# Outputs of six expert blocks as rows, with seven products of sums in place of eight

## The chip, the cores and the metric

The kernel runs on one core of a Trainium2 chip. Its engines work side by side, each through its own list of instructions in order: TensorE (PE, matrix products into PSUM; PEld is its loading of weights), VectorE (DVE), ScalarE (ACT), GpSimd (POOL) and SyncE (SP), with sixteen DMA engines for transfers. The metric is the device time of one execution in microseconds (us), the median of several runs. A profile is one more execution, recorded by the hardware.

## The reference

The program has two stages. The first is a linear attention with decay (4 sequences of 768 tokens, 8 heads of 48); its output, 3072 tokens of 384 numbers, is the input `x` of the second. The second sends every token to one of eight experts, and this is the stage that the change touches:

```python
# D = 384, E = 8 experts, F = 1024 hidden units, all float32
e = fresh_e if s == 0 or local_gate[b, s] < 0.5 else prev_e     # the token's expert
h = np.maximum(x[b, s] @ w1[e], 0.0)                            # 384 -> 1024
out[b, s] = p[e] * (h @ w2[e])                                  # 1024 -> 384, times the gate
```

## The kernel before

The routing gives each expert a list of tokens. Two experts first get small units of 192 slots; then come eight blocks, one for each expert, sorted by size. Each unit gathers the rows of its tokens, turns them (so that features lie on the partitions), computes hidden units in eight groups `m` of 128, and accumulates the outputs in PSUM.

```python
BLOCKS = (448, 424, 392, 376, 352, 336, 232, 192)     # slots of the eight blocks
P, D, DK, FK = 128, 384, 3, 8

def turn(self, i, j):              # 128 gathered rows of unit i -> exT   (L1033, L1034)
    tp = self.bank("etp")[:, :D].rearrange("p (k t) -> p k t", k=DK)
    for kk in range(DK):
        nc.tensor.transpose(tp[:, kk, :n], u["xg"][j][:n, kk * P:(kk + 1) * P], ...)
    nc.vector.tensor_copy(u["xT"][:, :, j * P:j * P + n], tp[:, :, :n])

def hidden(self, i, m):            # (L1047, L1051); hps has two banks
    for kk in range(DK):
        nc.tensor.matmul(h[:, :n], lhsT=u["w1"][:, m, kk, :], rhs=u["xT"][:, kk, :], ...)
    nc.scalar.activation(u[m], h[:, :n], Act.Relu)

def output(self, i, m):            # outputs with features on partitions   (L1059)
    for d in range(DK):
        nc.tensor.matmul(u["y"][d][:, :n], lhsT=u["w2"][:, m, d * P:(d + 1) * P], rhs=u[m], ...)

def drain(self, i):                # one copy on ScalarE, two on VectorE    (L1096)
    for d in range(DK):
        (nc.scalar.copy if d == 0 else nc.vector.tensor_copy)(u["yT"][:, d], u["y"][d][:, :n])

def send(self, i, j):              # 128 slots turned back into rows, scaled, scattered
    tp = self.bank("otp")[:, :D].rearrange("p (k t) -> p k t", k=DK)
    for d in range(DK):
        nc.tensor.transpose(tp[:n, d], u["yT"][:, d, j * P:j * P + n], self.ident)      # L1103
    nc.vector.tensor_scalar(yo[:n], tp..., u["gate"][:n, c:c + 1], None, Alu.mult)      # L1105
    nc.gpsimd.indirect_dma_start(out=..., in_=yo[:n], ...)                              # L1106
```

`bank` takes one of two PSUM banks in turn. The order in which the instructions are issued is written by hand:

```python
for i in range(n):                                  # units
    for m in range(FK):
        self.hidden(i, m)
        if sends and (m >= 1 if i > EARLY else i == EARLY and m >= 4):
            self.send(*sends.pop(0))                # rows of the unit before
        if m and i == n - 1:
            self.rows(m - 1)                        # last block: rows directly
        elif m:
            self.output(i, m - 1)                   # one step behind the hidden group
        ...                                         # [cut: routing at certain steps]
        if FK - after <= m:
            self.turn(i + 1, m - (FK - after))      # inputs of the unit to come
    if i < n - 1:
        self.output(i, FK - 1)
        self.drain(i)
        sends += [(i, j) for j in range(len(u["rows"]))]
```

The last block of 192 slots already computes its outputs as rows: 128 slots with the hidden units as weights and `w2` as the moving operand of 384 columns (L1067), and the remaining 64 slots as two halves of 192 columns that go to the two halves of the partitions (L1074).

Of the kernel before, what the change touches and what calls it, by code (L numbers as in the profile page):

```python
# [31 lines left out]
ST = 4  # L32
# [8 lines left out]

BLOCKS = (448, 424, 392, 376, 352, 336, 232, 192)
HALF = BLOCKS[-1] - P

FRESH_TO = -1.5 * 2.0 ** -23

# [505 lines left out]
class Router:  # L552
# [271 lines left out]

    def halves(self):

        nc, c = self.nc, (E - 1) * ST + 1
        tok, self.gateh, self.sidh = self.tl("tokh", [P, 1]), self.tl("gateh", [P, 1]), self.tl("sidh", [P, 1], I32)
        for g in range(2):
            z = slice(g * HALF, (g + 1) * HALF)  # L830
            nc.vector.tensor_copy(tok[z], self.tok2[:HALF, c:c + 1])
            nc.vector.tensor_copy(self.gateh[z], self.gate[:HALF, c:c + 1])
        none = self.tl("noneh", [P, 1])
        nc.vector.scalar_tensor_tensor(none, tok, 0.0, self.big, Alu.is_equal, Alu.mult)
        nc.vector.scalar_tensor_tensor(none, tok, 2.0, none, Alu.mult, Alu.add)
        nc.vector.tensor_tensor(self.sidh, none, self.side, op=Alu.add)

    def head(self, bank):
        tok = self.tok0.rearrange("p e j -> p (e j)")
# [122 lines left out]
class Experts:  # L962

    def __init__(self, tc, st, x_d, w1, w2, out, ident, router):
        self.tc, self.nc = tc, tc.nc
        self.x_d, self.w1, self.w2, self.ident, self.router = x_d, w1, w2, ident, router
        r = router  # L970

        def unit(e, slots, first, gid, sid, gate):
            n = -(-slots // P)
            return dict(e=e, n=slots, cols=list(range(first, first + n)), gid=gid, sid=sid, gate=gate,
                        rows=[min(P, slots - j * P) for j in range(n)])

        self.units = [unit(e, HEAD, 2 * e, r.gid0, r.sid0, r.gate0.rearrange("p e j -> p (e j)")) for e in range(EARLY)]
        self.units += [unit(None, n, b * ST, r.gid, r.sid, r.gate) for b, n in enumerate(BLOCKS)]

        self.outs = dram_disjoint_views(out, sum(len(u["cols"]) for u in self.units))  # L980
        self.gp = st.enter_context(tc.tile_pool(name="gp", bufs=6))
        self.wps = [st.enter_context(tc.tile_pool(name="wp0", bufs=1, reuse_waits="tile"))]

    def open(self, st):
        def pool(name, bufs, **kw):
            return st.enter_context(self.tc.tile_pool(name=name, bufs=bufs, reuse_waits="tile", **kw))

        self.wps.append(pool("wp1", 1))
        self.xp = pool("xp", 2)
        self.hp = pool("hp", 3)  # L990
        self.yp = pool("yp", 4)
        self.op = pool("op", 4)
        self.yps = pool("yps", 1, space=PSUM)
        self.hps = pool("hps", 2, space=PSUM)
        self.tps = pool("tps", 2, space=PSUM)

    def bank(self, name):
        return self.tps.tile([P, 512], F32, name=name, tag="tp")

    def fetch(self, i, engine):  # L1000
        u, wp = self.units[i], self.wps[i % 2]
# [40 lines left out]
    def hidden(self, i, m):  # L1042
        nc, u = self.nc, self.units[i]
        n = u["n"]
        h = self.hps.tile([P, 512], F32, name="h")
        for kk in range(DK):
            nc.tensor.matmul(h[:, :n], lhsT=u["w1"][:, m, kk, :], rhs=u["xT"][:, kk, :],  # L1047
                             start=(kk == 0), stop=(kk == DK - 1))
        last = i == len(self.units) - 1
        u[m] = self.hp.tile([P, n], F32, name="hL" if last else "hT", tag="hL" if last else "hT", bufs=FK if last else 3)  # L1050
        nc.scalar.activation(u[m], h[:, :n], Act.Relu)  # L1051

    def output(self, i, m):
        nc, u = self.nc, self.units[i]
        n = u["n"]
        if m == 0:
            u["y"] = [self.yps.tile([P, 512], F32, name=f"y{d}") for d in range(DK)]
        for d in range(DK):
            nc.tensor.matmul(u["y"][d][:, :n], lhsT=u["w2"][:, m, d * P:(d + 1) * P], rhs=u[m],  # L1059
                             start=(m == 0), stop=(m == FK - 1))  # L1060

    def rows(self, m):

# [14 lines left out]
    def send_rows(self, half):  # L1078
        nc, u, r = self.nc, self.units[-1], self.router
        n = D // 2 if half else D  # L1080
        c = u["cols"][0]
        gate, sid = (r.gateh, r.sidh) if half else (u["gate"][:, c:c + 1], u["sid"][:, c:c + 1])
        out = self.outs.pop()
        yo = self.op.tile([P, n], F32, name="yo", tag="yo")
        nc.vector.tensor_scalar(yo, u["y"][half][:, :n], gate, None, Alu.mult)
        nc.gpsimd.indirect_dma_start(  # L1086
            out=out.rearrange("n (h d) -> (n h) d", h=2) if half else out,
            out_offset=bass.IndirectOffsetOnAxis(ap=sid, axis=0),
            in_=yo, in_offset=None, bounds_check=(2 * N if half else N) - 1, oob_is_err=False)

    def drain(self, i):
        nc, u = self.nc, self.units[i]
# [5 lines left out]
    def send(self, i, j):  # L1098
        nc, u = self.nc, self.units[i]
        n, c = u["rows"][j], u["cols"][j]  # L1100
        tp = self.bank("otp")[:, :D].rearrange("p (k t) -> p k t", k=DK)
        for d in range(DK):
            nc.tensor.transpose(tp[:n, d], u["yT"][:, d, j * P:j * P + n], self.ident)  # L1103
        yo = self.op.tile([P, D], F32, name="yo", tag="yo")
        nc.vector.tensor_scalar(yo[:n], tp[:n].rearrange("p d x -> p (d x)"), u["gate"][:n, c:c + 1], None, Alu.mult)  # L1105
        nc.gpsimd.indirect_dma_start(  # L1106
            out=self.outs.pop(), out_offset=bass.IndirectOffsetOnAxis(ap=u["sid"][:n, c:c + 1], axis=0),
            in_=yo[:n], in_offset=None, bounds_check=N - 1, oob_is_err=False)

    def routing(self, s):  # L1110

        r, bank = self.router, self.bank
        if s == 0:
            r.experts_of(1)
            r.shares(1)
            r.gates(0)
        if s == 1:
            r.keys(1, bank("kp1"))
            r.runs(1)
            r.powers(1)  # L1120
        if s == 2:
            r.turn_runs(1, bank("rp1"))
        if s == 3:
            r.last(1, bank("bc1"))
            r.one_hot(1)
        if s == 4:
            r.counts(1, [bank("rk1"), bank("tt1")])
            r.ranks(1)
            r.blocks()
            r.slots(1)  # L1130
            r.columns(1)
            r.numbers(1)
            r.places(1, 0)
            r.places(1, 1)
        if s == 5:
            self.fetch(EARLY, self.nc.sync)
        if s == 7:
            r.summed(1, 0)
            r.copied(0)
        if s == 8:  # L1140
            r.tokens(bank("tb1"))
            self.gather(EARLY)
            r.gates(1)
            r.weights(0)
            r.weights(1)
        if s == 10:
            r.summed(0, 1)
        if s == 12:
            r.summed(1, 1)
            r.copied(1)  # L1150
        if s == 2 * FK:
            r.ends(bank("tb2"))
        if s == 2 * FK + 4:
            self.flag()

    def run(self, att, flag, ready):
        self.flag = flag
# [9 lines left out]
        for i in range(n):  # L1167
# [5 lines left out]
            for m in range(FK):  # L1173
                self.hidden(i, m)
                if i == 0 and m == 0:
                    att.turn(B * HP - 1, [self.bank("tp") for _ in range(2)])
                if sends and (m >= 1 if i > EARLY else i == EARLY and m >= 4):
                    self.send(*sends.pop(0))
                if m and i == n - 1:
# [9 lines left out]
            if i < n - 1:  # L1189
# [52 lines left out]
def kernel(  # L1242
# [41 lines left out]
    with ExitStack() as st, tc.manual_schedule():  # L1284
# [6 lines left out]
        ex.open(st)  # L1291
        router.open(1, st.enter_context(tc.tile_pool(name="ro1", bufs=1)))

        def flag():
# [7 lines left out]
            fp = router.mp  # L1302
# [79 lines left out]
```

## Time and profile before

The time is 406.2 us, the median of three runs from 405.75 to 406.56.

| what | value |
|---|---|
| span of the profiled execution | 404.0 us, mean TensorE clock 0.997 |
| TensorE busy | 391.1 us (97%) |
| VectorE busy | 145.2 us (36%) |
| ScalarE busy | 72.9 us (18%) |
| the block of 448 slots | 157.6 to 196.9 us |
| the blocks of 424, 392, 376 | start at 196.9, 233.8, 267.7 us |
| the blocks of 352, 336, 232 | start at 300.3, 330.6, 359.3 us |
| the last block, 192 | 380 us to the end |

How to read it: a line of the timeline gives the start and the duration in us, the engine, the line of the program (L1059), the operation, what it writes and reads, the shape, and how many instructions were merged into it. A line of a group gives, after the bar, busy time in us and mean ns of one instruction, and after the next bar the idle time of that engine directly before these instructions and who ended it. The duration of a matmul contains its run through the array, which overlaps with that of the next; how many fit into a stretch is read from the distance of the starts.

### The profile page before, as it was taken

Reading aid. Unit: us, or ns where it says so; the run is one execution under the profiler, and the core shown is the slowest. Engines: PE = TensorE matmul, PEld = TensorE weight load, DVE = VectorE, ACT = ScalarE, POOL = GpSimd, SP = SyncE. Lnnn points to the kernel's source line nnn. Section 1 sums busy time; section 2 is a strip of 40 time slices with the busy share of each in tenths; the row PEclk is TensorE's granted clock in tenths of the full one; section 3 lists DMA queues with packets and bytes.
Section 4 is the critical chain, followed back from the end, with each engine's and each line's share of the span. In section 5 each row is a group of like instructions: output and inputs, shape, how many; then the busy total and the mean of one; then the engine's idle time right before and its main releaser. Section 6 shows DMA issues by size and latency. Waiting matters only on the chain. (4 is left out here: it accounts for less than half of the span.)

```text
span 404.0 us, 8246 instructions
## 1 busy us (share of the span) xinstructions
PE 391.1 (97%) x3427; PEld 277.7 (69%) x3427; DVE 145.2 (36%) x321; ACT 72.9 (18%) x176; POOL 143.3 (35%) x179
## 2 busy tenths in 40 slices
PE   7999999899999999999999999999999999999992
PEld 6777786777769997555555555566666666689972
DVE  7887567678753723222211111121121011021200
ACT  4132222222222211110111111010111011111110
POOL 8679998786030060011424012302302302202011
PEclk9999999999999999999999999999999999999998
DMA  7999998988028766201922261272244144162011
GB/s 258 410 409 409 407 378 301 331 294 318 5 62 309 311 230 222 117 19 31 328 90 72 83 264 39 61 270 85 67 178 174 54 181 171 41 255 110 0 36 34
DMA packets 17468, 74.90 MB, mean 185 GB/s; under 512 B 2734, under 2 KB 6591, under 8 KB 14864
## 3 DMA queue, kind: packets, MB, share of 16 engines
q1 hardware_dynamic: 10048, 56.89, 37.2%
q0 software_dynamic: 3424, 9.54, 7.3%
q10 hardware_dynamic: 3952, 7.87, 5.3%
q8 instruction: 29, 0.48, 0.5%
q14 instruction: 15, 0.12, 0.1%
HBM read 64.85 MB, written 9.54 MB: 184 GB/s over the span
## 5 line engine op out<-in xcount | busy, mean ns | idle before, releaser
L1047 PE MATMUL h<-exT,w1t 128*128 128x192 f32 (+7 forms) x480 | 138.8, 428 | 0.0
L1059 PE MATMUL y<-hT,w2t 128*128 128x192 f32 (+7 forms) x432 | 131.3, 440 | 0.0
L1047 PEld LDWEIGHTS h<-exT,w1t 128*128 128x128 f32 x480 | 86.3, 190 | 37.4 <-issue 14.8
L1059 PEld LDWEIGHTS y<-hT,w2t 128*128 128x128 f32 x432 | 77.3, 190 | 31.9 <-issue 13.2
L1106 POOL DMA_INDIRECT out_dram<-yo,sid x27 | 26.8, 991 | 183.6 <-DVE yo L1105 159.7
L1051 ACT ACTIVATE hT<-h 128x192 f32<-128x192 f32 (+7 forms) x72 | 31.9, 443 | 199.6 <-PE h L1047 199.6
L1034 DVE COPY exT<-etp 128x384 f32<-128x384 f32 (+7 forms) x29 | 14.3, 495 | 98.4 <-PE etp L1033 98.4
L1105 DVE TENSOR_SCALAR yo<-otp,gate 128x384 f32<-128x384 f32 (+7 forms) x27 | 16.6, 616 | 91.6 <-PE otp L1103 91.6
L1020 POOL DMA_INDIRECT xg<-x_d,gid x29 | 29.7, 1023 | 45.7 <-DVE sm L869 25.8
L286 DVE TENSOR_TENSOR am<-pair,kept 128x768 f32<-128x768 f32 x32 | 30.1, 951 | 15.7 <-PE pair L284 15.2
L218 POOL TENSOR_TENSOR pd<-rk 128x384 f32<-128x384 f32 x32 | 31.9, 1020 | 3.1 <-DMA rk<-in_rk_dram 2.3
L293 PE MATMUL y<-am,kv 128*64 128x128 f32 x384 | 27.8, 278 | 1.9 <-issue 1.2
L214 POOL TENSOR_TENSOR ke<-kv,endT 128x288 f32<-128x288 f32 x32 | 25.0, 805 | 4.5 <-DMA kv<-in_kv_dram 3.5
L293 PEld LDWEIGHTS y<-am,kv 128*64 128x64 f32 x384 | 23.9, 136 | 3.0 <-issue 1.4
L231 POOL TENSOR_TENSOR rw<-rk,tab 128x384 f32<-128x384 f32 x26 | 23.6, 932 | 6.5 <-PE y L306 6.5
L284 PE MATMUL pair<-rw,kw 48*64 48x128 f32 (+1 forms) x768 | 22.5, 249 | 1.2 <-ACT end L165 0.6
L284 PEld LDWEIGHTS pair<-rw,kw 48*64 48x64 f32 x768 | 19.4, 133 | 2.6 <-issue 1.0
L310 ACT COPY xT<-y 128x768 f32<-128x768 f32 (+1 forms) x16 | 12.5, 779 | 40.7 <-PE y L306 40.7
L269 DVE TENSOR_TENSOR y<-y,vT 128x768 f32<-128x768 f32 x16 | 15.4, 962 | 3.7 <-PE y L265 3.5
L1033 PEld LDWEIGHTS etp<-ident,xg 128*128 128x128 f32 (+7 forms) x87 | 10.2, 140 | 8.2 <-issue 5.9
L238 DVE TENSOR_TENSOR kw<-rk,inv 128x768 f32<-128x768 f32 (+1 forms) x19 | 15.5, 818 | 0.1
L1103 PEld LDWEIGHTS otp<-ident,yT 128*128 128x128 f32 (+7 forms) x81 | 10.1, 132 | 7.7 <-issue 5.5
(214 smaller groups left out, 274.2 us busy)
## 6 DMA issues: line engine op xcount, KB each, us to landing
w1t<-in_w_dram SPq DMA_DIRECT2D x9, 1536.0 KB, 6.3
w2t<-in_w_dram SPq DMA_DIRECT2D x9, 1536.0 KB, 8.3
rk<-in_rk_dram SPq DMA_DIRECT2D x15, 768.0 KB, 9.3
kv<-in_kv_dram SPq DMA_DIRECT2D x16, 584.0 KB, 9.5
vT<-in_vT_dram SPq DMA_DIRECT2D x16, 384.0 KB, 7.5
x_d<-x ACTq DMA_DIRECT2D x4, 1152.0 KB, 11.3
w1t<-in_w_dram ACTq DMA_DIRECT2D x1, 1536.0 KB, 9.0
w2t<-in_w_dram ACTq DMA_DIRECT2D x1, 1536.0 KB, 12.3
```

The lines of the kernel that those rows point to most:

```text
L214: nc.gpsimd.tensor_mul(t["ke"][:, p::2], t["k"][:, p::2], spread(self.endT[:, p, hp], 1, C2))
L218: nc.gpsimd.tensor_mul(t["pd"][:, z], t["rT"][:, z], t["kT"][:, z])
L231: engine.tensor_mul(t["rw"][:, z], t["rT"][:, z], spread(pw, 1, z.stop - z.start))
L284: nc.tensor.matmul(sc[f * DP:(f + 1) * DP, h, i, x:], lhsT=t["kw"][q, c, o * DP:(o + 1) * DP], rhs=t["rw"][q, c, x:], start=True, stop=True)
L286: return lambda: nc.vector.tensor_mul(t["am"][:, g], sc, spread(self.kept[:, g:g + 3], 1, 2))
L293: nc.tensor.matmul(t["y"][p * DP:(p + 1) * DP, h, c2 * P:(c2 + 1) * P], lhsT=t["v"][:, (2 * c + h) * DH:(2 * c + h) * DH + DP], rhs=t["am" ...
L1020: self.nc.gpsimd.indirect_dma_start(out=xg[:n], out_offset=None, in_=self.x_d[:rows], in_offset=bass.IndirectOffsetOnAxis(ap=u["gid"][:n, ...
L1047: nc.tensor.matmul(h[:, :n], lhsT=u["w1"][:, m, kk, :], rhs=u["xT"][:, kk, :], start=(kk == 0), stop=(kk == DK - 1))
L1051: nc.scalar.activation(u[m], h[:, :n], Act.Relu)
L1059: nc.tensor.matmul(u["y"][d][:, :n], lhsT=u["w2"][:, m, d * P:(d + 1) * P], rhs=u[m], start=(m == 0), stop=(m == FK - 1))
L1105: nc.vector.tensor_scalar(yo[:n], tp[:n].rearrange("p d x -> p (d x)"), u["gate"][:n, c:c + 1], None, Alu.mult)
L1106: nc.gpsimd.indirect_dma_start(out=self.outs.pop(), out_offset=bass.IndirectOffsetOnAxis(ap=u["sid"][:n, c:c + 1], axis=0), in_=yo[:n], in ...
```

## The change

A product of two-by-two blocks, eight block products, can be made from seven, if sums of blocks are multiplied (Winograd's form of Strassen's scheme). The change uses it for the outputs of the six blocks of at least 336 slots: the first 256 slots in two halves of 128, the hidden groups in pairs, and the 384 output features in two halves of 192. The hidden units are the weights, so that the result has slots on the partitions, as rows. The slots beyond 256 are done in the ordinary way: as rows of 384 columns for up to 128 of them, as in the last block for 192 of them (448), and with features on the partitions, as before, for 168 and 136 of them (424 and 392). Rows need no turning back before they are scattered. What it is for: fewer columns through TensorE, and fewer transposes.

```diff
+PAIRS = 336
-        self.op = pool("op", 4)
+        self.op = pool("op", 5)
+        self.sp = pool("sp", 2)
+        self.jp = pool("jp", 1)
-        self.tps = pool("tps", 2, space=PSUM)
+        self.tp = [tps.tile([P, 512], F32, name=f"tp{i}") for i in range(2)]
     def bank(self, name):
-        return self.tps.tile([P, 512], F32, name=name, tag="tp")
+        if self.both:
+            self.tp.reverse()
+        return self.tp[0]                  # one bank from the first large block on
+    def sums(self, i, j):                  # four on VectorE, 128 x 128
+        for x, (a, b, op) in enumerate(((a21, a22, Alu.add), (t[:, 0], a11, Alu.subtract),
+                                        (a11, a21, Alu.subtract), (a12, t[:, 1], Alu.subtract))):
+            nc.vector.tensor_tensor(t[:, x], a, b, op=op)
+    def factors(self, i, j):               # four on VectorE, 128 x 192, of w2
+        for x, (a, b) in enumerate(((b12, b11), (b22, t[:, 0]), (b22, b12), (t[:, 1], b21))):
+            nc.vector.tensor_tensor(t[:, x], a, b, op=Alu.subtract)
+    def seven(self, i, j):                 # [cut]
+            u["hr"], u["y"] = y[3][:, half:D], self.tp[1]      # the rest takes the other bank
+        rest(m)
+        product(1, u[m][:, :P], h[:, m, :half])
+        rest(m + 1)
+        product(2, u[m + 1][:, :P], h[:, m + 1, :half])
+        product(4, u[m + 1][:, P:2 * P], t[:, 3])
+        product(5, s[:, 0], t[:, 0])
+        product(6, s[:, 1], t[:, 1])
+        product(7, s[:, 2], t[:, 2])
+        product(3, s[:, 3], h[:, m + 1, half:])
+    def join(self, i):                     # after the last pair
+        nc.scalar.copy(one, p(1))
+        nc.vector.tensor_tensor(u6, p(6), one, op=Alu.add)
+        ...                                # six more of 128 x 192 on VectorE
+        for x in range(2):
+            self.scaled(i, x, c[x], c[x])
+        if n <= P or n == P + HALF:
+            self.scaled(i, 2, u["y"][:, :D], ...)
+        ...                                # [cut: half rows of 448; yT of 424 and 392 on ScalarE]
+    def scaled(self, i, j, rows, yo):
+        self.nc.scalar.activation(yo[:n], rows[:n], Act.Copy, scale=u["gate"][:n, c:c + 1])
+        self.scatter(yo[:n], u["sid"][:n, c:c + 1])
@@ the order of issue
+                if u["seven"]:
+                    if m % 2:
+                        self.sums(i, m // 2)
+                        self.seven(i, m // 2)
+                        if m < FK - 1:
+                            self.factors(i, m // 2 + 1)
+                elif m and i == n - 1:
@@ [turn(i + 1, ...) follows here as before]
+            if i + 1 < n and self.units[i + 1]["seven"]:
+                self.factors(i + 1, 0)
+                self.both = False
+            if u["seven"]:
+                self.join(i)
+                if "yT" in u:
+                    sends += [(i, j) for j in range(2, len(u["rows"]))]
```

The indices and gates of half rows, which VectorE prepares at the end of the routing with seven small instructions for the last block, are now prepared for the 448 block too. A check on the decay values (`flag`), which used a bank of its own (`router.mp`), takes the bank for transposes, since `router.mp` now holds one of the seven products. The hidden tiles of the large blocks get four buffers (eight in the 448 block) in place of three.

More of the change, by code (lines that the diff above doesn't have):

```diff
@@ L825, in halves @@
     def halves(self):
[L827 to L836, printed above, removed]
+        nc, self.halved = self.nc, {}
+        for b in (0, E - 1):
+            c = b * ST + -(-BLOCKS[b] // P) - 1
+            tok, none = self.tl(f"tokh{b}", [P, 1]), self.tl(f"noneh{b}", [P, 1])
+            gate, sid = self.halved[b] = self.tl(f"gateh{b}", [P, 1]), self.tl(f"sidh{b}", [P, 1], I32)
+            for g in range(2):
+                z = slice(g * HALF, (g + 1) * HALF)
+                nc.vector.tensor_copy(tok[z], self.tok2[:HALF, c:c + 1])
+                nc.vector.tensor_copy(gate[z], self.gate[:HALF, c:c + 1])
+            nc.vector.scalar_tensor_tensor(none, tok, 0.0, self.big, Alu.is_equal, Alu.mult)
+            nc.vector.scalar_tensor_tensor(none, tok, 2.0, none, Alu.mult, Alu.add)
+            nc.vector.tensor_tensor(sid, none, self.side, op=Alu.add)
     def head(self, bank):
@@ L974, in unit @@
             return dict(e=e, n=slots, cols=list(range(first, first + n)), gid=gid, sid=sid, gate=gate,
+                        seven=slots >= PAIRS, rest=slots - 2 * P,
                         rows=[min(P, slots - j * P) for j in range(n)])
@@ L991, in open @@
         self.yp = pool("yp", 4)
-        self.op = pool("op", 4)
+        self.op = pool("op", 5)
+        self.sp = pool("sp", 2)
+        self.jp = pool("jp", 1)
         self.yps = pool("yps", 1, space=PSUM)
         self.hps = pool("hps", 2, space=PSUM)
-        self.tps = pool("tps", 2, space=PSUM)
+        tps = pool("tps", 1, space=PSUM)
+        self.tp = [tps.tile([P, 512], F32, name=f"tp{i}") for i in range(2)]
+        self.both = True
     def bank(self, name):
-        return self.tps.tile([P, 512], F32, name=name, tag="tp")
+        if self.both:
+            self.tp.reverse()
+        return self.tp[0]
     def fetch(self, i, engine):
@@ L1048, in hidden @@
                              start=(kk == 0), stop=(kk == DK - 1))
-        last = i == len(self.units) - 1
-        u[m] = self.hp.tile([P, n], F32, name="hL" if last else "hT", tag="hL" if last else "hT", bufs=FK if last else 3)
+        last = i == len(self.units) - 1 or u["seven"] and u["rest"] == P + HALF
+        u[m] = self.hp.tile([P, n], F32, name=f"hL{n}" if last else "hT", tag=f"hL{n}" if last else "hT", bufs=FK if last else 4)
         nc.scalar.activation(u[m], h[:, :n], Act.Relu)
@@ L1060, in output @@
                              start=(m == 0), stop=(m == FK - 1))
+    def sums(self, i, j):
+        nc, u = self.nc, self.units[i]
+        (a11, a21), (a12, a22) = [[u[2 * j + k][:, x * P:(x + 1) * P] for x in range(2)] for k in range(2)]
+        u["s"] = t = self.sp.tile([P, 4, P], F32, name="sums")
+        for x, (a, b, op) in enumerate(((a21, a22, Alu.add), (t[:, 0], a11, Alu.subtract),
+                                        (a11, a21, Alu.subtract), (a12, t[:, 1], Alu.subtract))):
+            nc.vector.tensor_tensor(t[:, x], a, b, op=op)
@@ new lines, in factors, with product, rest @@
+    def factors(self, i, j):
+        nc, u = self.nc, self.units[i]
+        (b11, b12), (b21, b22) = [[u["w2"][:, 2 * j + k, x * D // 2:(x + 1) * D // 2] for x in range(2)] for k in range(2)]
+        u["t", j] = t = self.sp.tile([P, 4, D // 2], F32, name="factors")
+        for x, (a, b) in enumerate(((b12, b11), (b22, t[:, 0]), (b22, b12), (t[:, 1], b21))):
+            nc.vector.tensor_tensor(t[:, x], a, b, op=Alu.subtract)
+    def seven(self, i, j):
+        nc, u = self.nc, self.units[i]
+        n, h, half = u["rest"], u["w2"], D // 2
+        if j == 0:
+            y = [self.yps.tile([P, 512], F32, name=f"y{d}") for d in range(DK)] + [self.router.mp]
+            u["p"] = {k: (y[x // 2], x % 2) for x, k in enumerate((1, 2, 4, 5, 6, 7, 3))}
+            u["hr"], u["y"] = y[3][:, half:D], self.tp[1]
+        def product(k, a, b):
+            bank, x = u["p"][k]
+            nc.tensor.matmul(bank[:, x * half:(x + 1) * half], lhsT=a, rhs=b, start=(j == 0 and x == 0),
+                             stop=(j == FK // 2 - 1), skip_group_check=True)
+        def rest(m):
+            first, last = m == 0, m == FK - 1
+            if n <= P or n == P + HALF:
+                z = min(n, P)
+                nc.tensor.matmul(u["y"][:z, :D], lhsT=u[m][:, 2 * P:2 * P + z], rhs=h[:, m], start=first, stop=last)
+            else:
+                for d in range(DK):
+                    nc.tensor.matmul(u["y"][:, d * n:(d + 1) * n], lhsT=h[:, m, d * P:(d + 1) * P], rhs=u[m][:, 2 * P:],
+                                     start=(first and d == 0), stop=last, skip_group_check=True)
+        m, s, t = 2 * j, u["s"], u["t", j]
+        rest(m)
[7 more added lines that the diff above has]
+        product(3, s[:, 3], h[:, m + 1, half:])
+        if j == FK // 2 - 1 and n == P + HALF:
+            for m in range(FK):
+                for g in range(2):
+                    nc.tensor.matmul(u["hr"][g * HALF:(g + 1) * HALF], lhsT=u[m][:, 3 * P:],
+                                     rhs=h[:, m, g * half:(g + 1) * half], start=False, stop=(m == FK - 1), skip_group_check=True)
@@ new lines, in join, with p @@
+    def join(self, i):
+        nc, u = self.nc, self.units[i]
+        n, half = u["rest"], D // 2
+        def p(k):
+            bank, x = u["p"][k]
+            return bank[:, x * half:(x + 1) * half]
+        t = self.jp.tile([P, 3, half], F32, name="t")
+        c = [self.op.tile([P, D], F32, name="yo", tag="yo") for _ in range(2)]
+        one, u6, z = t[:, 0], t[:, 1], t[:, 2]
+        nc.scalar.copy(one, p(1))
+        nc.vector.tensor_tensor(u6, p(6), one, op=Alu.add)
+        nc.vector.tensor_tensor(c[0][:, :half], p(2), one, op=Alu.add)
+        nc.vector.tensor_tensor(z, p(7), u6, op=Alu.add)
+        nc.vector.tensor_tensor(u6, p(5), u6, op=Alu.add)
+        nc.vector.tensor_tensor(c[1][:, :half], z, p(4), op=Alu.subtract)
+        nc.vector.tensor_tensor(c[1][:, half:], p(5), z, op=Alu.add)
+        nc.vector.tensor_tensor(c[0][:, half:], p(3), u6, op=Alu.add)
+        for x in range(2):
+            self.scaled(i, x, c[x], c[x])
+        if n <= P or n == P + HALF:
+            self.scaled(i, 2, u["y"][:, :D], self.op.tile([P, D], F32, name="yo", tag="yo"))
+            if n > P:
+                yo, (gate, sid) = self.op.tile([P, D], F32, name="yo", tag="yo")[:, :half], self.router.halved[i - EARLY]
+                nc.scalar.activation(yo, u["hr"], Act.Copy, scale=gate)
+                self.scatter(yo, sid, True)
+        else:
+            u["yT"] = self.yp.tile([P, DK, n], F32, name="yT", tag="yT")
+            nc.scalar.copy(u["yT"].rearrange("p d n -> p (d n)"), u["y"][:, :DK * n])
@@ new lines, in scaled, with scatter @@
+    def scaled(self, i, j, rows, yo):
+        u = self.units[i]
+        n, c = u["rows"][j], u["cols"][j]
+        self.nc.scalar.activation(yo[:n], rows[:n], Act.Copy, scale=u["gate"][:n, c:c + 1])
+        self.scatter(yo[:n], u["sid"][:n, c:c + 1])
+    def scatter(self, yo, sid, half=False):
+        out = self.outs.pop()
+        self.nc.gpsimd.indirect_dma_start(
+            out=out.rearrange("n (h d) -> (n h) d", h=2) if half else out,
+            out_offset=bass.IndirectOffsetOnAxis(ap=sid, axis=0),
+            in_=yo, in_offset=None, bounds_check=(2 * N if half else N) - 1, oob_is_err=False)
@@ L1081, in send_rows @@
         c = u["cols"][0]
-        gate, sid = (r.gateh, r.sidh) if half else (u["gate"][:, c:c + 1], u["sid"][:, c:c + 1])
-        out = self.outs.pop()
-        yo = self.op.tile([P, n], F32, name="yo", tag="yo")
+        gate, sid = r.halved[E - 1] if half else (u["gate"][:, c:c + 1], u["sid"][:, c:c + 1])
+        yo = self.op.tile([P, D], F32, name="yo", tag="yo")[:, :n]
         nc.vector.tensor_scalar(yo, u["y"][half][:, :n], gate, None, Alu.mult)
[L1086 to L1089, printed above, removed]
+        self.scatter(yo, sid, half)
     def drain(self, i):
@@ L1101, in send @@
         tp = self.bank("otp")[:, :D].rearrange("p (k t) -> p k t", k=DK)
+        first = j * P - (2 * P if u["seven"] else 0)
         for d in range(DK):
-            nc.tensor.transpose(tp[:n, d], u["yT"][:, d, j * P:j * P + n], self.ident)
+            nc.tensor.transpose(tp[:n, d], u["yT"][:, d, first:first + n], self.ident)
         yo = self.op.tile([P, D], F32, name="yo", tag="yo")
         nc.vector.tensor_scalar(yo[:n], tp[:n].rearrange("p d x -> p (d x)"), u["gate"][:n, c:c + 1], None, Alu.mult)
-        nc.gpsimd.indirect_dma_start(
-            out=self.outs.pop(), out_offset=bass.IndirectOffsetOnAxis(ap=u["sid"][:n, c:c + 1], axis=0),
-            in_=yo[:n], in_offset=None, bounds_check=N - 1, oob_is_err=False)
+        self.scatter(yo[:n], u["sid"][:n, c:c + 1])
     def routing(self, s):
@@ L1153, in routing @@
         if s == 2 * FK + 4:
-            self.flag()
+            self.flag(bank("fp"))
     def run(self, att, flag, ready):
@@ L1178, in run @@
                     self.send(*sends.pop(0))
-                if m and i == n - 1:
+                if u["seven"]:
[5 more added lines that the diff above has]
+                elif m and i == n - 1:
                     self.rows(m - 1)
@@ L1188, in run @@
                     self.turn(i + 1, m - (FK - after))
-            if i < n - 1:
+            if i + 1 < n and self.units[i + 1]["seven"]:
[5 more added lines that the diff above has]
+                    sends += [(i, j) for j in range(2, len(u["rows"]))]
+            elif i < n - 1:
                 self.output(i, FK - 1)
@@ L1292, with flag @@
         router.open(1, st.enter_context(tc.tile_pool(name="ro1", bufs=1)))
-        def flag():
+        def flag(fp):
             ok = ro.tile([P, 2, HP], F32, name="ok")
@@ L1301, in flag @@
             nc.vector.tensor_reduce(some, ok[:, 0], axis=AX.X, op=Alu.add)
-            fp = router.mp
             nc.tensor.matmul(fp[:1, :1], lhsT=some, rhs=router.ones[:, 0:1], start=True, stop=True)
```

## Prediction

> **What bounds the kernel now.** I read the page first (busy shares, then the 40 slices), then the groups by line with shapes kept apart, then the waits, then the timeline of single stretches. The chain of waits was no help: it has two pieces, both at the very end.
>
> ```profile
> PE 391.1 (97%) x3427; PEld 277.7 (69%) x3427; DVE 145.2 (36%) x321; ACT 72.9 (18%) x176; POOL 143.3 (35%) x179
> PE   7999999899999999999999999999999999999992
> ...
> L1059 PE MATMUL y<-hT,w2t 128*128 128x192 f32 (+7 forms) x432 | 131.3, 440 | 0.0
> L1105 DVE TENSOR_SCALAR yo<-otp,gate 128x384 f32<-128x384 f32 (+7 forms) x27 | 16.6, 616 | 91.6 <-PE otp L1103 91.6
> ```
>
> TensorE is busy 97% of the span and the output matmuls (L1059) have 0.0 us of idle time in front of them, while VectorE and ScalarE wait for TensorE. So any time taken from TensorE's stream comes off the end, and any wait put into it is added. A matmul of the program appears as two records (10 units x 8 x 3 hidden matmuls give x480). A busy TensorE is not yet TensorE at its pace, so I took the pace from the distance between starts.
>
> ```profile
> 219.89 2.30 PE L1059 MATMUL y<-hT,w2t 128*128 128x424 f32 x6
> 222.02 0.49 PE L1033 MATMUL etp<-ident,xg 128*128 128x128 f32 x3
> 222.35 2.30 PE L1047 MATMUL h<-exT,w1t 128*128 128x424 f32 x6
> 222.55 0.56 DVE L1034 COPY exT<-etp 128x384 f32<-128x384 f32 x1 [4.04 <-PE etp L1033]
> ...
> 389.08 0.81 PE L1067 MATMUL y<-w2t,hL 128*128 128x384 f32 x2
> 389.72 1.14 PE L1047 MATMUL h<-exT,w1t 128*128 128x192 f32 x6
> 390.70 0.81 PE L1067 MATMUL y<-w2t,hL 128*128 128x384 f32 x2
> ```
>
> Six records of 424 columns take 222.02 - 219.89 = 2.13 us (0.356 each), six of 192 take 0.98 (0.163), two of 384 take 0.64 (0.32), a group of three transposes 0.33. All lie on p(n) = 0.833 n + 3 ns. There is no minimum at 192 columns: the 190 ns of a weight load are hidden. VectorE's copy of transposes starts 0.53 us after the first of them, 0.2 us after their last slot.
>
> ```profile
> 194.22 0.38 PE L1033 MATMUL etp<-ident,xg 40*128 40x40 f32 x3
> 194.53 2.52 PE L1059 MATMUL y<-hT,w2t 128*128 128x448 f32 x6
> 196.89 3.37 PE L1047 MATMUL h<-exT,w1t 128*128 128x424 f32 x9
> ```
>
> This is the border of two blocks. Between the last transposes of the next block's inputs and the first hidden matmul that reads them lie 2.36 us of output matmuls, which hide the copy. Keep this in mind.
>
> [...]
>
> **The change part by part.**
>
> *Columns.* Before, outputs of a block of n slots are 48 records of n columns: 48 p(n) = 18.06, 17.10, 15.82, 15.18, 14.22, 13.58 us for n = 448 to 336, sum 94.0. After: seven products x 4 pairs x 2 records = 56 records of 192, 56 x 0.163 = 9.13 us a block, 54.8 for six. (The 256 slots alone cost 48 x 0.833 x 256 = 10.24 before, so a block gains 1.1.) The rest of the slots: for 376, 352 and 336 16 records of 384 columns whatever the number of slots, 5.17 us each, against 4.80, 3.84 and 3.20 for 120, 96 and 80 slots; for 424 and 392 48 records of 168 and 136 columns, 6.86 and 5.58; for 448 5.17 plus 32 half-width records, which in the last block now take (2.82 - 0.33)/31 = 0.08 us each because two run side by side, 2.6. Sum 35.7. Total 90.5: the products win only **3.4 us**, because 352 and 336 lose what they win.
>
> *Transposes of outputs.* Row outputs need no turning back: 4 + 2 + 2 + 3 + 3 + 3 = 17 of 27 groups go, 17 x 0.33 = **5.6 us**. Gain in TensorE's stream together: **9.0 us**.
>
> *Border, first wait (A).* In the built order of the changed kernel, the last transposes of the next block's inputs stand directly before its first hidden matmul, because the seven products of the last pair are issued before them and nothing remains for afterwards. So TensorE waits 0.2 us (to the copy's start) + copy + about 0.17 (signal and weight load). The copies are 0.28 us for 40 slots and 0.18 for 8 in the trace; for 120, 96, 80 and 104 slots I read 0.53, 0.45, 0.40, 0.47 from the 0.36 and 0.56 at 64 and 128 slots. Sum over six borders 6 x 0.37 + 2.3 = **4.5 us**.
>
> *Border, second wait (B).* ScalarE takes the scaling of three row groups into its queue ahead of the next block's first Relu. [...] Counting from the transposes' last slot, with c the copy: sums complete at 0.2 + c + 1.3 + 2.25 = c + 3.75; ScalarE's scaling 0.6 + 0.5 + 0.5 to c + 5.4 (448 has a fourth, c + 5.8); Relu 0.4, signal 0.2: c + 6.0. TensorE meanwhile has only two hidden groups after wait A, ready at c + 0.37 + 12 p(n'): c + 4.65 for 424, 4.66 and 4.5 for 392 and 376 (with one send), 3.9 and 3.8 for 352 and 336. The border to 232 has no factors: c + 4.6 against c + 2.7. Waits 1.8, 1.35, 1.4, 2.05, 2.2, 1.85: **10.6 us**. Before, one ScalarE copy and two VectorE copies were all, and two hidden groups hid them.
>
> *Inside the 448 block (C).* Its first sums stand behind the routing's end on VectorE, which runs to 164.17 us in the trace and gets 1.0 us longer; the fifth product is due at 162.23 + 2.28 = 164.5 and gets its sum near 165.65: 1.15. With one transpose bank, the flag's matmul waits for the send's scaling and four small operations, and the next transposes for the flag's reader: 0.2 + 1.16 + 0.15 + 0.3 + 0.15 + 0.15 - 0.1 = 2.0. At the seventh step a send and a turn meet in the bank: 0.95. Together **4.1 us**.
>
> [...]
>
> Sum: -9.0 + 4.5 + 10.6 + 4.1 = **+10.2 us**, 406.2 + 10.2 = 416.4.
>
> **The rivals.** First: the gain arrives whole, since TensorE was the bound and VectorE is idle in these blocks (its digit is 0 to 2 in most slices): 397 us. Against it stands the built order, in which TensorE's next work needs a copy that begins only then. Second: the join is hidden as drains are today and only A and C are paid: 406.2 - 9.0 + 8.6 = 406. For it: 3.4 to 4.3 us of hidden matmuls at each border. [...]
>
> **Range and chances.** The gain is sure to about 1 us, A and C to 1.5 each. B is weakest: 0.5 us more or less per border moves the result by 3, and it could fall to half if neighbours overlap more than I count. I predict **416 us**, 80% between **409** and **421**. Faster by over 2% (below 398) would need no wait at all: 0.06. Slower by over 2% (above 414.3): 0.6. Within 2%: 0.34.
>
> **What would show it.** Right: the six first hidden groups have 0.5 to 0.9 us of TensorE idle before them, released by VectorE's exT; the first rest matmul of the next block has 1.3 to 2.2 us, released by ScalarE's hT; the 448 block shows gaps near its fifth product and at the flag; paces stay on p(n). Wrong: gaps at borders under 1 us in sum (then B is hidden), 192-column products slower than 0.17 us each, or gaps inside every pair.

## The result and the profile after

The changed kernel took 410.5 us (median of 4 runs, 410.0 to 411.3) against 406.1 us of the kernel before (median of 4): a ratio of 1.0109, 95% interval 1.0088 to 1.0131. It is slower by 4.4 us, 1.1%. The prediction had said 416 us, slower by 10.2 us.

The page of the changed kernel, engines, slices and the TensorE groups of the blocks (in the slices each digit is the busy share of a fortieth of the span, in tenths; in the groups the last figures are the idle time before and who ended it):

```profile
PE 384.6 (94%) x3616; PEld 298.5 (73%) x3616; DVE 191.5 (47%) x533; ACT 80.4 (20%) x195; POOL 143.8 (35%) x179
...
PE   7999999999999999989899999989989989989992
...
L1061 PE MATMUL h<-exT,w1t 128*128 128x192 f32 (+7 forms) x480 | 138.2, 429 | 2.9 <-DVE exT L1048 2.9
...
L1074 PE MATMUL y<-hT,w2t 128*128 128x192 f32 (+1 forms) x144 | 29.3, 340 | 1.2 <-ACT hT L1066 1.2
L1106 PE MATMUL y<-factors,sums 128*128 128x192 f32 x144 | 27.4, 327 | 0.7 <-DVE sums L1084 0.7
...
L1113 PE MATMUL tp<-w2t,hT 128*120 128x384 f32 (+2 forms) x48 | 19.7, 491 | 2.8 <-ACT hT L1066 2.8
```

TensorE is busy for 6.5 us less than before (384.6 against 391.1), although it has 189 records more, and the span is 4.3 us longer. Eights stand among its nines, in the half of the span where the blocks lie. The idle time in front of its groups, 0.0 before, now has names: VectorE's copy of inputs (exT), ScalarE's Relu (hT), VectorE's sums. All TensorE waits from the 448 block on, longest first (total us, times, longest):

```profile
PE h L1061 <- DVE exT L1048: 2.9, 6, 0.6
PE tp L1113 <- ACT hT L1066: 2.8, 2, 1.5
PE tp L1429 <- DVE some L1428: 1.2, 1, 1.2
PE y L1074 <- ACT hT L1066: 1.2, 1, 1.2
PE tp L1219 <- ACT yT L1165: 1.2, 2, 0.7
PE tp L1116 <- ACT hT L1066: 1.0, 1, 1.0
PE tp L1047 <- DVE yo L1221: 0.7, 1, 0.7
PE y L1106 <- DVE sums L1084: 0.7, 1, 0.7
PE tp L1047 <- DVE over L1430: 0.2, 1, 0.2
```

Six waits for the copy and six for ScalarE (2 + 1 + 2 + 1) are the two waits at each of the six borders. At 424 to 392 and 392 to 376 the one that waits for ScalarE is a send of the block before: its transposes need `yT`, which ScalarE copies after the two scalings and ahead of the Relu. The other four are inside the 448 block: the flag, its reader, the send that shares the bank, the first sums. These figures leave out the last record's own run through the array (a record of 192 columns lasts 0.33 us, the next one starts after 0.16), during which no new record starts, so the loss is larger than their sum of 11.9 us.

How long each block lasts, from its first hidden matmul to that of the next (the last column ends with TensorE's last record):

| kernel | 448 | 424 | 392 | 376 | 352 | 336 | 232 and 192 | all |
|---|---|---|---|---|---|---|---|---|
| before | 39.28 | 36.94 | 33.90 | 32.58 | 30.30 | 28.73 | 37.2 | 238.95 |
| after | 42.10 | 36.08 | 33.89 | 32.78 | 31.66 | 30.96 | 37.8 | 245.31 |

The 448, 352 and 336 blocks lose, 424 wins a little, 392 stays, 376 loses slightly. In sum the part of the program that changed is **6.4 us** longer, not 4.4. The profiled executions differ by 2.0 us ahead of it: the 448 block starts at 157.61 us before and at 155.58 after. The first experiment looks at that.

One border in the changed kernel's timeline, 376 to 352 (start and duration in us):

```profile
299.46 0.41 PE L1047 MATMUL tp<-ident,xg 96*128 96x96 f32 x3
...
299.91 0.46 DVE L1048 COPY exT<-tp 128x288 f32<-128x288 f32 x1 [2.23 <-PE tp L1047]
300.29 0.35 DVE L1092 TENSOR_TENSOR factors<-w2t 128x192 f32<-128x192 f32 x1
300.43 3.82 PE L1061 MATMUL h<-exT,w1t 128*128 128x352 f32 x12 [0.55 <-DVE exT L1048]
...
301.49 0.35 DVE L1148 TENSOR_TENSOR t<-y,t 128x192 f32<-128x192 f32 x1
...
303.20 0.35 DVE L1154 TENSOR_TENSOR yo<-mp,t 128x192 f32<-128x192 f32 x1
303.58 1.12 ACT L1171 ACTIVATE yo<-yo,gate 128x384 f32<-128x384 f32 x2 [5.23 <-DVE yo L1154]
...
304.61 0.56 ACT L1171 ACTIVATE yo<-tp,gate 120x384 f32<-120x384 f32 x1
305.07 0.80 ACT L1066 ACTIVATE hT<-h 128x352 f32<-128x352 f32 x2
305.57 0.89 PE L1113 MATMUL tp<-w2t,hT 128*96 128x384 f32 x2 [1.33 <-ACT hT L1066]
```

Read it as one chain: transposes, copy, four factors (300.29 to 301.49), seven additions of the join (to 303.55), three scalings (to 305.07), the Relu that had long been possible, and only then TensorE again. TensorE has two groups of hidden matmuls in the meantime, which end near 304.1.

### The profile page after: what moved, and what is told of

The parts are those of the page before. It is cut to its first block, busy times and chain, and to the rows that moved or that the text cites. A ratio compares the mean times of both kernels' runs of the same rounds, so it can differ in the third digit from the quotient of the medians.

```text
span 408.3 us, 8809 instructions
## 1 busy us (share of the span) xinstructions
PE 384.6 (94%) x3616; PEld 298.5 (73%) x3616; DVE 191.5 (47%) x533; ACT 80.4 (20%) x195; POOL 143.8 (35%) x179
## 5 line engine op out<-in xcount | busy, mean ns | idle before, releaser
L1061 PEld LDWEIGHTS h<-exT,w1t 128*128 128x128 f32 x480 | 85.3, 190 | 35.6 <-issue 12.7
L1066 ACT ACTIVATE hT<-h 128x192 f32<-128x192 f32 (+6 forms) x64 | 26.8, 428 | 140.9 <-PE h L1061 140.9
L1048 DVE COPY exT<-tp 128x384 f32<-128x384 f32 (+7 forms) x29 | 14.3, 494 | 68.0 <-PE tp L1047 68.0
L1084 DVE TENSOR_TENSOR sums<-hT 128x128 f32<-128x128 f32 x40 | 11.5, 288 | 60.3 <-ACT hT L1066 60.3
L1074 PE MATMUL y<-hT,w2t 128*128 128x192 f32 (+1 forms) x144 | 29.3, 340 | 1.2 <-ACT hT L1066 1.2
L1106 PE MATMUL y<-factors,sums 128*128 128x192 f32 x144 | 27.4, 327 | 0.7 <-DVE sums L1084 0.7
L1074 PEld LDWEIGHTS y<-hT,w2t 128*128 128x128 f32 x144 | 24.9, 190 | 2.0 <-ACT hT L1066 1.6
L1106 PEld LDWEIGHTS y<-factors,sums 128*128 128x128 f32 x144 | 24.0, 190 | 1.0 <-DVE sums L1084 1.0
L1113 PE MATMUL tp<-w2t,hT 128*120 128x384 f32 (+2 forms) x48 | 19.7, 491 | 2.8 <-ACT hT L1066 2.8
L1106 PE MATMUL y<-w2t,hT 128*128 128x192 f32 x80 | 19.6, 326 | 0.0
```

The costliest lines, as they stand in the source:

```text
L1106: nc.tensor.matmul(bank[:, x * half:(x + 1) * half], lhsT=a, rhs=b, start=(j == 0 and x == 0), stop=(j == FK // 2 - 1), skip_group_check=True)
```

## The experiments

The traces give a measure that is far finer than the times: the lengths of undisturbed blocks repeat to 0.01 or 0.02 us from one execution to the next, while the times of one kernel spread by several us on some chips (20 runs of one variant on one chip: 408.0 to 413.3 us). So each variant is judged by its ratio to the kernel before on the same chip, and by the lengths of its blocks.

**The two kernels again.** No edit.

> The kernel before, unchanged, once more. It settles a side question: the profile of before has TensorE waiting 1.2 us for nothing visible at 73.4 us, in the attention stage, which the profile of the changed kernel has not; its expert blocks start 2.0 us earlier. If that pause belongs to the kernel before (its own build), it is there again at the same place and the 448 block starts near 157.6 us. If it was chance of one execution, the block starts near 155.6 us and the pause is gone, and the changed kernel's loss is 2 us larger than its blocks alone explain.

> The changed kernel, unchanged, beside its variants on one chip. In the traces the six blocks last 201.7 us before (twice, to 0.01 us) and 207.5 after, and the rest of TensorE's work after them 37.2 and 37.8: 6.4 us in sum, while the times differ by 4.4. If the missing 2.0 us were an advantage of the changed kernel in the attention stage, the ratio is again 1.011. If they were chance of the few runs, it comes nearer to 1.016.

Measured: the kernel before again lasts 238.95 us from the first hidden group of 448 to TensorE's end, and its block starts at 161.14 us. Neither of the two expected starts came. It paused in other places: TensorE waited in front of L293 for 0.57 us at 72.73 us and 2.15 us at 114.19 us, and once in the first experts. The first line is from the first execution of the kernel before, the second from the repeat:

```profile
73.44 1.47 PE L293 MATMUL y<-am,kv 128*64 128x128 f32 x20 [1.19 <-issue]
```

```profile
150.78 1.24 PE L1059 MATMUL y<-hT,w2t 128*128 128x192 f32 x6 [2.03 <-ACT hT L1051]
```

The first pause is shorter and the second is new, in the same code. Over all twelve profiled executions of this study the 448 block starts between 155.6 and 163.4 us, and the start goes with the chip more than with the kernel: 155.8 to 157.7 us on one chip, 160.1 to 160.4 on a second, 161.1 to 163.4 on a third. A difference of 2.0 us is within what one chip shows. With four runs of the changed kernel and fifteen of the kernel before on one chip the changed one stands at 1.0166 (1.0133 to 1.02), 411.4 us against 405.1, and its blocks repeat: 42.08, 36.08, 33.89, 32.78, 31.67, 30.96. What has to be explained is 6.4 us; the ratio of 1.0109 was probably low by the 2 us by which the two executions differ ahead of the blocks. What makes the pauses is open.

**The last transposes ahead of the last products**, at all borders but 448 to 424.

```diff
+                early = u["seven"] and m == FK - 1 and i > EARLY
+                if early:
+                    self.turn(i + 1, m - (FK - after))
                 if u["seven"]:
                     if m % 2:
                         self.sums(i, m // 2)
...
-                if FK - after <= m:
+                if FK - after <= m and not early:
```

> The last transposes of the next block's inputs are issued ahead of the seven products of the last pair, at five of the six borders. Theory (both waits at a border are one chain: copy of exT, factors, join, scaling, Relu): the first wait goes and VectorE makes the factors under the products, so that the second wait shrinks too; each border gains 1.1 to 1.5 us, the last 0.45: 5.5 us, 405.0. Rival (the waits are independent): only the first wait goes, 3.0 to 3.5 us, 407. Second rival (the second wait is counted from the last product, whatever the copy does): the first wait passes into the second and nothing is gained, 410.5.

Measured: ratio 0.9975 (0.9949 to 1.0); first hidden group of 448 to TensorE's end 238.31 us, 7.0 less than the changed kernel, where 5.5 had been expected. At the five borders the first waits are gone; of the second ones those of 424 to 392 and 392 to 376 are gone, those of 376 to 352 and 352 to 336 shrink, and the one before 232, where no factors are made, stays. The same border in this kernel:

```profile
303.52 0.49 PE L1106 MATMUL mp<-w2t,sums 128*128 128x192 f32 x2
303.79 0.36 DVE L1148 TENSOR_TENSOR t<-y,t 128x192 f32<-128x192 f32 x1 [0.74 <-PE y L1106]
303.84 3.71 PE L1061 MATMUL h<-exT,w1t 128*128 128x352 f32 x12
...
307.88 0.89 PE L1113 MATMUL tp<-w2t,hT 128*96 128x384 f32 x2 [0.33 <-ACT hT L1066]
```

The factors are made under the products, and the join's first addition now waits for TensorE (0.74 us), the other way round than before. It starts before the last product (mp) is through, since it needs only the sixth and the first. From the end of the last product's slot (303.84) to TensorE's restart pass 4.04 us; in the changed kernel 5.14 us pass from its first hidden group to the restart (300.43 to 305.57). Both waits are one chain; the two rivals (3.5 us, nothing) fall.

**The join ahead of the factors.**

```diff
             if i + 1 < n and self.units[i + 1]["seven"]:
-                self.factors(i + 1, 0)
                 self.both = False
             if u["seven"]:
                 self.join(i)
+            if i + 1 < n and self.units[i + 1]["seven"]:
+                self.factors(i + 1, 0)
+            if u["seven"]:
```

> The join stands ahead of the next block's four factors on VectorE; nothing else is changed. Theory (the second wait is the chain through VectorE): sums are complete 1.2 us earlier, the waits of 1.14, 0.8, 0.87, 1.48 and 1.63 us shrink to 0 to 0.4, the border to 232 stays as it is: 5.2 us, 405.3. Rival (ScalarE's four or five operations alone make the wait, VectorE is done in time): no change, 410.5. Possible price: the factors come late for the fourth product, which would show as a wait for VectorE there.

Measured: ratio 1.0000 (0.9974 to 1.0026), 239.82 us, 5.5 less than the changed kernel's 245.31. The second waits are gone but for idle times of 0.13 us at the border to 352, 0.27 at that to 336 and the unchanged 1.23 before 232; no wait for factors appears. VectorE's place in the chain is real: the four factors take 1.2 us ahead of the join, and the 352 and 336 blocks, whose second waits were longer than that, are each 1.20 us shorter (30.47 and 29.76).

**The scaling behind the Relus.**

```diff
-        for x in range(2):
-            self.scaled(i, x, c[x], c[x])
+        self.late = [lambda x=x: self.scaled(i, x, c[x], c[x]) for x in range(2)]
...
+                if m == 1:                       # after hidden(i, 1) and its Relu
+                    for what in self.late:       # the half rows of 448 come first
+                        what()
+                    self.late = []
```

> ScalarE scales the two joined row groups (and the half rows of 448) only after the next block's first two Relus; the remaining rows, which need no join, are scaled at once. Theory (the second wait is the Relu's place in ScalarE's queue behind work that waits for VectorE): the second waits of 7.3 us in sum go, plus about 0.5 for weight loads after a wait; 403.0. Rival (TensorE waits for the PSUM banks that VectorE's join still reads): the wait moves to the first product and about half stays, 407.

Measured: ratio 1.0017 (0.9991 to 1.0042), 240.54 us in the trace. No wait for ScalarE is left at any border, so the second wait was a place in ScalarE's queue, that of the Relu (at 424 to 392 and 392 to 376 that of the copy `yT`); the rival (PSUM banks) falls. In this execution a pause struck the border 448 to 424 (below), so 424 and 448 can't be used: together they are 3.1 us longer than in the run before, which is why the trace gains 4.8 us where the theory had 7.8. The theory's 0.5 us for weight loads was an estimate: behind the wait at 376 to 352 of the changed kernel two records of 384 columns take 0.73 us (305.57 to 306.30), without a wait 0.64. Whether the pause struck the other executions too is not shown. The other blocks give the two waits apart: 32.98, 31.81, 30.09, 29.26 and 36.3 after them. Against the changed kernel that is a second wait of 0.91, 0.97, 1.58, 1.70 and 1.50 us. That of 448 to 424 is read from the run before this one, where it is gone: 36.08 - 34.88 = 1.20 us.

**Both together.** The edits of the first and the last of these.

> Both changes of order together: the last transposes ahead of the last pair's products at five borders, and the scaling of joined rows after the next block's first two Relus. Theory: no wait is left at a border but the first one at 448 to 424 (0.44 us); the six blocks last 198 us, the ratio to the kernel before is 0.989. Rival (a third chain, the PSUM banks that the join reads, takes over): waits of 0.5 us or more for VectorE's join before the first product of a block, ratio 0.995.

Measured: ratio 0.9891 (0.9849 to 0.9932), 399.7 us. Blocks 42.09, 34.59, 32.10, 31.01, 29.35, 28.42. The border 376 to 352:

```profile
295.25 0.49 PE L1106 MATMUL mp<-w2t,sums 128*128 128x192 f32 x2
...
295.57 3.71 PE L1061 MATMUL h<-exT,w1t 128*128 128x352 f32 x12
...
297.59 0.46 ACT L1066 ACTIVATE hT<-h 128x352 f32<-128x352 f32 x1 [2.65 <-issue]
...
299.12 0.81 PE L1113 MATMUL tp<-w2t,hT 128*96 128x384 f32 x2
299.37 0.46 ACT L1066 ACTIVATE hT<-h 128x352 f32<-128x352 f32 x1 [1.31 <-PE h L1061]
299.73 1.11 ACT L1174 ACTIVATE yo<-yo,gate 128x384 f32<-128x384 f32 x2
```

TensorE goes from the last product to the hidden groups and on to the next outputs without a bracket of idle time; the scalings stand behind both Relus. The difference of a block here and in the run before is the first wait: 0.88, 0.80, 0.74, 0.84 us at the end of 392, 376, 352, 336. For 424 the run with the join first serves: 34.88 - 34.59 = 0.29 us.

**The 448 block alone**, on the changed kernel.

```diff
         self.exceeded()
-        self.halves()
...
-        if s == 2 * FK + 4:
+        if s == 2 * FK + 2:
             self.flag(bank("fp"))
+            r.halves()
...
-                if sends and (m >= 1 if i > EARLY else i == EARLY and m >= 4):
+                if sends and (m >= 1 if i > EARLY else i == EARLY and m >= 3 and m % 2):
```

> Only the three edits inside the 448 block, on the changed kernel (flag earlier, sends at odd steps, half rows' indices after the first sums); all border waits stay. Theory: the waits of that block are independent of the borders, it lasts 42.1 - 3.5 - 0.3 = 38.3 us, and the changed kernel gains 3.5 us: ratio 1.007 if the changed kernel stands at 1.016. Rival: the time of this block passes into the next border; then 1.012.

Measured: ratio 1.0069 (1.0044 to 1.0095). The block lasts 38.30 us in place of 42.10; 0.33 of the 3.80 is a send that went to the next block, where it falls into the border's wait (the Relu's wait there is 0.66 in place of 0.98). The block's own waits cost 3.5 us, and nothing of it comes back.

**Everything moved.** Both border edits and those of the 448 block; then the border 448 to 424 as well (the first condition without `i > EARLY`, sends of the 448 block at steps 3 and 5).

> As the run before, and inside the 448 block the flag is computed two steps earlier, the sends stand only at odd steps from the third, and the half rows' indices come after the first sums. Theory: the waits of 0.86, 1.7 and 0.87 us in that block go as well, TensorE runs without a gap as in the kernel before, and the whole reduction of its stream is left: ratio 0.980. Rival: one of them was hidden behind another and comes back elsewhere in the block, ratio 0.985.

> As the version with everything moved, and the last border (448 to 424) has its last transposes ahead of the last products too; two sends go to the next block for it. Theory: no wait of TensorE is left in the six blocks; from the first hidden group of 448 to TensorE's end it takes 238.95 - 9.0 = 229.9 us (the version before this one: 230.3), ratio 0.977. Rival: the copy of exT was hidden nowhere and the wait appears at a send: 230.3 again.

Measured: 0.9784 (0.9741 to 0.9826), 396.5 us, 230.33 us in the blocks; and 0.9775 (0.974 to 0.9809), 399.4 us on another chip, 230.09 us. The 448 and 424 blocks together last 73.23 and 72.98 us: the border between them gained 0.25 us of the 0.4 expected. The second page:

```profile
PE   7999999999999999999999999999999999999992
...
L1060 PE MATMUL h<-exT,w1t 128*128 128x192 f32 (+7 forms) x480 | 138.1, 428 | 0.0
...
L1105 PE MATMUL y<-factors,sums 128*128 128x192 f32 x144 | 27.3, 326 | 0.0
```

The nines stand in a row again and the idle time before the groups is 0.0. These two take 2.2% less than the kernel before (by their intervals 1.7 to 2.6%); the first took 396.5 us on the chip on which the changed kernel took 411.4. What is left, 238.95 - 230.09 = 8.9 us, is the whole reduction of TensorE's stream.

**Four blocks in place of six.**

```diff
-PAIRS = 336
+PAIRS = 376
```

> The seven products only for the four blocks of 376 slots and more; 352 and 336 are computed as before. Theory (columns of these two blocks rise by 0.06 and 0.71 us, six groups of transposes are saved, 2.0 us, and their borders cost some 6 us): leaving them out gains 4.9 us on the changed kernel, ratio 1.004. Rival (the products themselves are worth it in every block): it loses 1 us or more against the changed kernel.

Measured: ratio 1.0064 (1.0037 to 1.0091), 240.59 us in the blocks, 4.7 less than the changed kernel on the same measure, near the 4.9 of the theory. As issued, the products of 352 and 336 cost more than they save. Without waits it is the other way round: 29.35 and 28.42 us against 30.30 and 28.73 of the kernel before, though their columns rise.

## Why the prediction was wrong in size

The mechanism was right: less work for TensorE, two waits at each border, and waits inside the 448 block. The sum of the waits was too large, and 2 us came from ahead of the blocks.

| term | predicted | measured | from |
|---|---|---|---|
| columns and transposes | -9.0 | -8.9 | the version without waits against before |
| first wait at six borders (A) | 4.5 | 3.8 | block by block, see below |
| second wait at six borders (B) | 10.6 | 7.9 | block by block, see below |
| inside the 448 block (C) | 4.1 | 3.5 | the 448 block alone |
| sum, in the blocks | 10.2 | 6.4 | 245.31 - 238.95 (rounded terms give 6.3) |
| ahead of the blocks | 0 | -2.0 | not the change's, gone in the repeat |

*TensorE's stream* was sized to 0.1 us. The products of 192 columns take 0.163 us a record, and six records of 136 columns take 0.69 us (247.00 to 247.69): p(n) held in shapes that the kernel before did not have.

*The step that failed is B*, "Waits 1.8, 1.35, 1.4, 2.05, 2.2, 1.85: 10.6 us". Measured: 1.20, 0.91, 0.97, 1.58, 1.70, 1.50: 7.9. Each border is too high by 0.35 to 0.6 us, because the chain on VectorE and ScalarE is shorter than I added up. At 376 to 352, from the last slot of the transposes (299.71): sums complete after 3.84 us where I had 4.20 (factors 1.20 for 1.3, additions 2.06 for 2.25, and the copy and the first factor overlap by 0.08); scaling 1.49 for 1.6; Relu to TensorE 0.50 for 0.6. Independent neighbours on VectorE start 0.26 to 0.28 us apart though each lasts 0.35; those that need their neighbour's result (300.29 and 300.67), or overwrite what it reads (302.02 and 302.40), start 0.38 apart. The terms of this sum for the four factors (1.3 us), the seven additions (2.25) and the scaling of joined rows (0.6) are estimates that no run shows; the trace of the changed kernel has 1.20, 2.06 and 0.607 us. A wait is a small difference of two large sums (here 5.9 us of chain, 4.4 us of cover), so 0.5 us in the chain was a third of the wait. The chance of slower by over 2%, 0.6, rested on this excess.

Two signs that the prediction named came only in part. Of the second waits' idle times, 0.98, 0.57, 0.65, 1.33, 1.47 and 1.23 us, four lie below its 1.3 to 2.2. And where it counted a send as cover (424 to 392, 392 to 376), the send itself waited.

*A* was right at the four borders with 80 to 120 slots in the last transposes: 0.88, 0.80, 0.74, 0.84 us against 0.90, 0.82, 0.77, 0.84 predicted. At the two with 40 and 8 slots it was too high: 0.25 and 0.29 us against 0.65 and 0.55, and the idle times there (0.38 and 0.28 us) lie below its 0.5 to 0.9. The 0.17 us for signal and weight load in each of these waits no run shows: from the end of the copy to the hidden matmul pass 0.06 us at 376 to 352 (300.37 to 300.43). Part of such a wait is not regained by moving the transposes: behind the 8-slot ones, six records of 168 columns take 0.96 us in place of 0.86. *C* was right in its three parts and 0.6 us too high in sum; moving three calls removed it as one piece, which didn't pass on to the next border.

*The rivals.* "The gain arrives whole" was wrong for the change as issued and right for the version with the order mended. "The join is hidden and only A and C are paid" is refuted by the waits for ScalarE. Inside the pairs VectorE was in time: in all of the changed kernel's blocks there is one wait for sums, the first (0.7 us).

## What to carry to other kernels

When TensorE is full, count the waits that a change puts at the seams before counting what it saves: here 8.9 us were saved and 15.2 us of waits paid, 11.7 of them at the seams, and a mere reordering of the same instructions turned +1.7% into -2.2%. At a seam, write down each engine's queue in order; work that must follow a late result (scaling behind a join) goes behind work that TensorE needs next (Relu), and transposes go ahead of the last matmuls, so that their copy has cover. Size such a wait with start-to-start distances from a trace, not with durations, since it is a small difference of large sums.

## What the runs showed of the hardware that I had not expected

In the execution with the scaling behind the Relus, TensorE paused for about 2 us at the border 448 to 424 and then ran at half pace. The windows of that trace around the pause (busy us and instructions per engine, then the granted TensorE clock, the DMA share and GB/s):

```profile
202.70:204.90 2.20, 0.39 (x5) 0.26 (x3) 0.32 (x2) 0.00 (x0) 1.59 (x3) 1.00 0.55 164
204.90:208.90 4.00, 3.99 (x7) 2.01 (x8) 3.07 (x11) 0.00 (x0) 1.05 (x1) 0.57 0.93 343
208.90:211.00 2.10, 2.10 (x8) 1.10 (x7) 0.00 (x0) 0.52 (x1) 0.00 (x0) 1.00 0.48 195
```

In the 4.0 us after the pause the granted clock is 0.57 on average, and twelve hidden records take 6.07 us to the next group (204.91 to 210.98) in place of 4.28, so a pause of 2 us was followed by another 1.8 us of loss. The waits of 1.5 us and less at the borders of the changed kernel did not have this effect (in the 4 us behind the second waits of 1.33 and 1.47 us, from 305.57 and 337.22 us on, the granted clock is 1.00). Length alone doesn't decide it: ahead of the blocks, behind an idle time of 2.05 us in the run with the join first, six records of 192 columns take 1.52 us (151.45 to 152.97); behind one of 2.03 us such six records take 1.17 us in the repeat of the kernel before (150.78 to 151.95) and as much in the run with the scaling behind the Relus (151.02 to 152.19). What caused the pauses was not tried.
